# ScalarE's hi parts first in each slot, VectorE's lo parts last, and the first batch's keys on GpSimd: a pooled attention with a gated expert layer

## The chip, the core and the metric

The kernel runs on one core of one Trainium2 chip. The metric is the device time of one launch in microseconds (us), the median of several runs. All work goes through five engines, each with an instruction queue that it works off strictly in order: PE (TensorE: matrix products and transpositions into PSUM; its weight loads are listed as PEld), DVE (VectorE), ACT (ScalarE, which also issues some DMAs), POOL (GpSimd) and SP (SyncE, which here only issues DMAs).

## The reference

Attention against keys and values that are averaged over 8 positions (72 pooled keys for 576 queries, 8 batches, 8 heads, 64 wide), and then a gated layer without a nonlinearity:

```python
k_p = k.reshape(B, H, Sp, pool, D).mean(axis=3)
v_p = v.reshape(B, H, Sp, pool, D).mean(axis=3)
scores = scale * np.matmul(q, k_p.transpose(0, 1, 3, 2))
scores = scores - np.max(scores, axis=-1, keepdims=True)
attn = np.exp(scores)
attn = attn / (np.sum(attn, axis=-1, keepdims=True) + 1e-09)
attn_out = np.matmul(attn, v_p)
x = attn_out.transpose(0, 2, 1, 3).reshape(B * S, H * D)      # 4608 x 512
a = x @ w1;  b = x @ w2                                       # 512 -> 1024
out = (a * b @ w3) @ w_out                                    # 1024 -> 1024 -> 512
```

All inputs and outputs are float32.

## The kernel before

**Splitting.** A float32 operand of a product is kept as a hi part (a rounded copy, nearly always written by ACT) and a lo part (the operand minus hi, written by DVE, sometimes by GpSimd). A product is three passes: hi x hi, hi x lo, lo x hi. So nearly each result that PE leaves in PSUM is read twice, by ACT for hi and by DVE for lo.

**Stages.** (1) *The opening* builds W = w3 x w_out (its first half) in 8 steps, `w_block(v)` and `w_mm(s, ...)`. The weights arrive as 32-bit halves of 64-bit numbers: `high` (ACT) and `low` plus the two operations of `conv_b` (DVE) rebuild a float32 in the tile `wt`; `w_turn` transposes on PE, and a hi/lo pair `hl` is made of the transposed w3 and of w_out. Beside it runs the attention of chunk 0. (2) *The middle* goes over 12 chunks of 384 tokens. For chunk m and column block j of 4, `a_mm` and `b_mm` are 12 products each (w1 and w2), `a_post` and `b_post` make g = a x b and its hi part, `g_lo` the lo part, and `out_mm` multiplies by W into three accumulators `o`, which `out_post(m, t)` copies out through `ob` and stores as a partial result. In the same slots stands the attention of the next chunk. (3) *The tail* adds the other half of the hidden width by another scheme (lines 730 and 797) and stores the output.

**Attention of one chunk n**, tile t of 96 or 128 tokens: `s_mm` (scores of four heads each, `att` in PSUM), `soft1` (maximum, subtraction, exponential; where the pair (n, t) is in SOFT_ACT, ACT does the subtraction and the sum too), `soft2` (division), `soft3` (the 8 keys that don't fit 64, as tile R in hi and lo), `pt_mm` and `ptr_mm` (transpositions), `pt_post` and `ptr_post` (their evictions PTh, PTl, PTr), `av_mm` (times v) and `av_post` (xT hi and lo for the next layer, and a copy `xs` that is stored for the tail). PSUM tiles named `att` share three buffers; a buffer is given again when its last reader is through. For batch b, `load_k` and `prep_k` sum the keys over 8 positions, by a tree of three additions on GpSimd or, for the pairs in K_DVE, by one reduction on DVE; `kt_mm` and `kt_post` make `kbd` of them; `prep_v`, `prep_v2`, `prep_vr` and `prep_vr2` do the same for v, where `prep_vr` holds three ACT operations that wait for GpSimd's sum, and `prep_v2` an ACT copy `vbd` that GpSimd's queue then waits for. `st` (three buffers) takes the loads of k and v, `qs` (four) those of q, and `tr_q` on DVE frees a `qs`.

**What sets the order.** A plan written as numbers. `at(kind, k, fn, ...)` puts a call at slot k. Calls are run sorted by whole slot, then by kind in the order L (loads), P (work on ACT, DVE and GpSimd), M (main products), A (attention products), then by the fraction of k. So each engine's queue holds the work of slot after slot, and within a slot's P part the fraction decides. M0 is the slot of `a_mm` of chunk 0, and a chunk has IA = 12 slots. `plan_att`, `plan_kv` and `plan_q` place one chunk's attention, one batch's keys and values, and one chunk's queries:

```python
plan.append((k // 1, "LPMA".index(kind), k % 1, len(plan), fn, args))
...
for _, _, _, _, fn, args in sorted(plan, key=lambda x: x[:4]):
    fn(*args)
```

An instruction that reads a PSUM tile on one engine also waits for an earlier reader of the tile on another engine.

Of the kernel before, what the change touches and what calls it, by code (L numbers as in the profile page):

```python
# [19 lines left out]
def kernel(  # L20
# [170 lines left out]

    def w_block(v):


# [1 line left out]
        if new:
            w_tiles(v)
            r3, z3 = stage["w3", v]
            ro, zo = stage["wo", v]
            high(raw["w3", v], z3)  # L200
            low(raw.pop(("w3", v)), r3)
            high(raw["wo", v], zo)
        if old:
            s = v - 2
            sub(wo[s][1], f(stage["wo", s][0]), f(wo[s][0]))
        if new:
            if v > 0:
                low(raw["wo", v], ro)
            conv_b(r3, z3)
        if mid:  # L210
            ps = w_turn(v - 1)
            w3t[v - 1] = hl(cell, 8 + (v - 1) % 4)
            nc.scalar.copy(out=w3t[v - 1][0], in_=ps)
        if new:
            if v == 0:
                low(raw["wo", v], ro)
            conv_b(ro, zo)
        if mid:
            wo[v - 1] = hl(cell, v - 1)
            nc.scalar.copy(out=wo[v - 1][0], in_=f(stage["wo", v - 1][0]))  # L220
        if mid:
            nc.vector.tensor_tensor(out=w3t[v - 1][1], in0=ps, in1=f(w3t[v - 1][0]), op=ALU.subtract)
# [267 lines left out]
    def soft1(n, t, half):  # L490
# [9 lines left out]
        if (n, t) not in SOFT_ACT:  # L500
            nc.vector.tensor_tensor(  # L501
                out=E[:nt, hs], in0=sv,
                in1=mx[:nt, hs].unsqueeze(2).broadcast_to([nt, 4, KP]), op=ALU.subtract)
            nc.scalar.activation(out=E[:nt, hs], in_=E[:nt, hs], func=AF.Exp, scale=-1.0)  # L504
            nc.vector.reduce_sum(out=sm[:nt, hs], in_=E[:nt, hs], axis=AX.X)  # L505
            return
# [50 lines left out]
    def pt_post(n, t):  # L557
# [26 lines left out]
    def av_post(n, pr):  # L584
# [235 lines left out]
    def plan_att(n, k, s_at, pt_at, av_at):  # L820


        for t in range(len(tok_tiles(n))):
# [98 lines left out]
    for u in range(8):
# [4 lines left out]
        at("A", k + 2, w2_turn, u)  # L927
        at("P", k + 3, w2_split, u)
        at("A", k + 4, w2_mm, u)
        at("P", k + 5, w2_post, u)  # L930
# [79 lines left out]
```

## Time and profile before

| | us |
|---|---|
| median of 3 runs | 932.97 (930.59 to 935.16) |
| the profiled execution | 934.14 |
| its span, first to last instruction | 932.0 |
| opening, to the first `a` product | 121.4 |
| chunk 0 of the middle | 54.6 |
| chunks 1 to 11 | 478 |
| tail | 278 |
| PE busy | 797.7 (86%) |
| DVE busy | 615.4 (66%) |
| ACT busy | 340.8 (37%) |
| POOL busy | 240.7 (26%) |

The mean granted TensorE clock is 0.937 of full speed. One load of a key pair is 288 KB, one step of W loads 512 KB of w3 and 512 KB of w_out, one query DMA is 48 KB. In the profile, an engine is busy while it works on an instruction; a wait is named by what released it, and since queues are in order, a wait delays all that stands behind it on its engine. A wait on an engine that others don't wait for costs nothing.

### The profile page before, as it was taken

The numbers are of one execution on the slowest core, as the hardware profiler recorded it, in microseconds if no ns is written. First come the engines' busy times: TensorE is split into PE (matmuls) and PEld (weight loads), VectorE is DVE, ScalarE is ACT, GpSimd is POOL, SyncE is SP. The second block draws the span as 40 slices with busy tenths as digits, with TensorE's granted clock in tenths as the row PEclk, the third lists the DMA queues.
The fourth block names the chain that finished last, engine by engine and source line by source line (L and its number), as shares of the span: only waits on it lengthen the run. The fifth ranks groups of instructions, "written<-read, shape, count | busy, mean of one in ns | idle before, by whom it ended". The sixth has DMA issues, their size and how long they took to land.

```text
span 932.0 us, 12974 instructions
## 1 busy us (share of the span) xinstructions
PE 797.7 (86%) x4512; PEld 720.2 (77%) x4512; DVE 615.4 (66%) x1273; ACT 340.8 (37%) x863; POOL 240.7 (26%) x295
## 2 busy tenths in 40 slices
PE   3466667898889897979997988998899999999998
PEld 3344556887778796868886877887898998998996
DVE  2968578656565756485765676657777687677644
ACT  2244452453444443433443443544222122122111
POOL 2644137344151342422251100000211211211211
PEclk7767879799899998999998999999899999999999
DMA  8954523444444444424433312253141341341122
GB/s 242 242 125 139 149 56 87 112 129 117 102 113 106 130 119 112 116 89 107 133 80 90 95 56 80 74 192 128 44 141 58 108 142 57 108 142 57 58 91 79
DMA packets 131840, 102.56 MB, mean 110 GB/s; under 512 B 82624, under 2 KB 103104, under 8 KB 130752
## 3 DMA queue, kind: packets, MB, share of 16 engines
q1 hardware_dynamic: 116800, 81.82, 32.6%
q10 hardware_dynamic: 14976, 19.93, 6.0%
q8 instruction: 35, 0.57, 0.3%
q14 instruction: 29, 0.24, 0.1%
HBM read 72.35 MB, written 29.36 MB: 109 GB/s over the span
## 4 chain that ended last, share of the span: by engine, by line
PE 40%; DVE 28%; ACT 14%; DMA 9%; issue 4%; POOL 2%; ACTq 2%; SPq 1%; DVEq 0%; POOLq 0%
PE ps L730 19%; PE att L797 11%; PE att L282 3%; ACT E L504 2%; DMA st<-in_v_dram 2%; PE a L609 2%; DVE E L501 2%; DVE mx L499 2%; DVE PTl L566 2%; DVE sm L505 2%; PE o L644 2%; DVE xT L126 2%; DVE gl L635 2%; DVE a L629 2%; DMA qs<-in_q_dram 2%
## 5 line engine op out<-in xcount | busy, mean ns | idle before, releaser
L730 PE MATMUL ps<-xo,sw 128*128 128x288 f32 x1344 | 182.3, 297 | 3.5 <-ACT m L749 3.5
L730 PEld LDWEIGHTS ps<-xo,sw 128*128 128x128 f32 x1344 | 181.7, 190 | 4.4 <-ACT m L749 3.7
L742 POOL TENSOR_TENSOR g<-g,u 128x288 f32<-128x288 f32 x48 | 40.8, 866 | 339.9 <-DVE u L123 339.9
L644 PE MATMUL o<-W,gh 128*128 128x512 f32 x288 | 95.6, 414 | 27.6 <-ACT ob L649 26.3
L609 PE MATMUL a<-xT,hl 128*128 128x384 f32 x576 | 115.8, 350 | 2.7 <-ACT hl L181 1.5
L441 POOL TENSOR_TENSOR st<-st 72x512 f32<-72x512 f32 (+1 forms) x54 | 74.2, 1374 | 166.5 <-DMA st<-in_v_dram 56.1
L609 PE MATMUL b<-xT,hl 128*128 128x384 f32 x576 | 113.2, 344 | 2.1 <-DVE a L629 1.2
L609 PEld LDWEIGHTS a<-xT,hl 128*128 128x128 f32 x576 | 105.5, 197 | 5.2 <-POOL hl L182 1.9
L609 PEld LDWEIGHTS b<-xT,hl 128*128 128x128 f32 x576 | 100.8, 192 | 3.1 <-POOL hl L182 1.6
L644 PEld LDWEIGHTS o<-W,gh 128*128 128x128 f32 x288 | 51.6, 192 | 41.4 <-ACT ob L649 32.7
L797 PE MATMUL att<-W,gh 128*128 128x512 f32 x256 | 80.2, 394 | 0.0
L483 PE MATMUL att<-kbd,qT 128*128 128x144 f32 (+1 forms) x320 | 60.6, 314 | 21.5 <-ACT xs L594 10.1
L483 PEld LDWEIGHTS att<-kbd,qT 128*128 128x128 f32 (+1 forms) x320 | 50.6, 195 | 30.6 <-ACT xs L594 11.3
L504 ACT ACTIVATE E<-E 128x288 f32<-128x288 f32 (+1 forms) x70 | 31.1, 444 | 107.7 <-DVE E L501 103.1
L123 DVE TENSOR_TENSOR u<-u,ps 128x288 f32<-128x288 f32 x112 | 49.0, 451 | 18.1 <-PE ps L730 17.9
L505 DVE TENSOR_REDUCE sm<-E 128x4 f32<-128x288 f32 (+1 forms) x70 | 31.6, 451 | 41.7 <-ACT E L504 41.7
L644 PE MATMUL o<-W,gl 128*128 128x512 f32 x144 | 58.1, 403 | 0.8 <-DVE gl L635 0.8
L749 ACT COPY m<-ps 128x288 f32<-128x288 f32 x32 | 12.8, 400 | 123.4 <-PE ps L730 110.0
L797 PEld LDWEIGHTS att<-W,gh 128*128 128x128 f32 x256 | 48.0, 188 | 10.9
L566 DVE TENSOR_TENSOR PTl<-att,PTh 128x512 fp32r<-128x512 f32 (+1 forms) x40 | 25.4, 636 | 43.7 <-ACT PTh L565 43.5
L126 DVE TENSOR_TENSOR xT<-att,xT 128x384 fp32r<-128x384 f32 x48 | 26.7, 556 | 41.0 <-ACT xT L589 40.6
L797 PE MATMUL att<-W,gl 128*128 128x512 f32 x128 | 50.5, 394 | 0.0
(126 smaller groups left out, 1421.5 us busy)
## 6 DMA issues: line engine op xcount, KB each, us to landing
raw<-in_moe_w_dram SPq DMA_DIRECT2D x32, 512.0 KB
st<-in_k_dram SPq DMA_DIRECT2D x32, 288.0 KB
pd<-ob ACTq DMA_DIRECT2D x36, 256.0 KB
x<-xd SPq DMA_DIRECT2D x8, 1152.0 KB
part<-pd SPq DMA_DIRECT2D x36, 256.0 KB
out_dram<-ob SPq DMA_DIRECT2D x36, 256.0 KB
st<-in_v_dram SPq DMA_DIRECT2D x32, 256.0 KB
qs<-in_q_dram SPq DMA_DIRECT2D x128, 48.0 KB
```

Source lines behind the costliest of these rows:

```text
L123: eng.tensor_tensor(out=out, in0=a, in1=b, op=ALU.add)
L126: eng.tensor_tensor(out=out, in0=a, in1=b, op=ALU.subtract)
L441: nc.gpsimd.tensor_tensor(out=t[:, :, 0:4], in0=t[:, :, 0:4], in1=t[:, :, 4:8], op=ALU.add)
L483: nc.tensor.matmul(out=ps[:nt, 2 * KP * j:2 * KP * (j + 1)], lhsT=qT[n][:, pr, off:off + nt], rhs=kbd[b % 2][:, pr], start=True, stop=True,)
L504: nc.scalar.activation(out=E[:nt, hs], in_=E[:nt, hs], func=AF.Exp, scale=-1.0)
L505: nc.vector.reduce_sum(out=sm[:nt, hs], in_=E[:nt, hs], axis=AX.X)
L566: nc.vector.tensor_tensor(out=lo, in0=pv[:, :, :nt], in1=f(hi), op=ALU.subtract)
L609: nc.tensor.matmul(out=o, lhsT=w12[j, w][sw][:, kt * P:(kt + 1) * P], rhs=x[sx][:, kt], start=(i == 0), stop=(i == 3 * NK - 1))
L644: nc.tensor.matmul(out=oacc[m][t], lhsT=(gh, gl)[sg][:, c], rhs=W[0, j][sw_], start=(j == 0 and i == 0), stop=(j == NA - 1 and i == 2))
L730: nc.tensor.matmul(out=ps[:, :HS], lhsT=w[a][:, kt * P:(kt + 1) * P], rhs=x[b][:, kt], start=(j == 0), stop=(j == 5))
L742: nc.gpsimd.tensor_tensor(out=d, in0=d, in1=tmp[into], op=ALU.mult)
L797: nc.tensor.matmul(out=oacc["b", no], lhsT=G[no][a][:, j], rhs=W[1, j][b], start=(j == 0 and n == 0), stop=(j == 3 and n == 2))
```

## The change

In every slot, the P part is put in another order, and some calls are cut in two so that it can be:

- `av_post` now holds the hi copy, the `xs` copy and its store; the lo part is a call of its own, `av_lo`, behind them. `pt_post` keeps the hi copy, `pt_lo` is new. `b_post` is now the product alone, `g_hi` and `g_lo` follow. `soft3` keeps ACT's copies, `soft4` has DVE's subtractions, and `soft2`, `soft3` and `soft4` of a tile stand in one slot. The two sums of E per tile become one, in `soft2`.
- `w_block` is reordered: ACT's hi copies of the step before first, then per matrix the lo part and the rebuilding. The `high` operations go into `w_high`, a slot earlier.
- Key pair 1 of batch 0 leaves K_DVE, so all four are summed on GpSimd. The first three key loads stand behind four steps of W's loads, queries behind the fifth step, the fourth key pair and the values later.
- Numbers: M0 is a slot later (K0 + 3), attention of chunk 0 starts at slot 10 in place of 7, that of chunk 1 moves as well; `out_post` of a chunk's second and third accumulator moves from one and two slots behind the first to 0.4 and 1; `w2_turn` and `w2_split` are one slot later, `w2_mm` and `w2_post` two.

```diff
-    K_DVE = [(0, 1), (1, 1)]
+    K_DVE = [(1, 1)]
...
+    def w_high(v):
+        w_tiles(v)
+        high(raw["w3", v], stage["w3", v][1])
+        high(raw["wo", v], stage["wo", v][1])
...
     def soft2(n, t):
...
+        if (n, t) not in SOFT_ACT:
+            nc.vector.reduce_sum(out=sm[:nt], in_=E[:nt], axis=AX.X)
...
+    def soft4(n, t):
+        nt = tok_tiles(n)[t][2]
+        R = Rt[n, t][:nt]
         for dup in range(2):
-            nc.vector.tensor_tensor(
-                out=R[:nt, :, :, dup, 1], in0=er, in1=f(R[:nt, :, :, dup, 0]), op=ALU.subtract)
+            sub(R[:, :, :, dup, 1], rest_keys(n, t), f(R[:, :, :, dup, 0]))
...
         nc.scalar.copy(out=xh, in_=ps)
-        sub(xl, ps, f(xh))
+        stage["xl", n, pr] = xl, ps, f(xh)
...
+    def av_lo(n, pr):
+        sub(*stage.pop(("xl", n, pr)))
...
-            at("P", k + av_at[pr] + 1, av_post, n, pr)
+            at("P", (k + av_at[pr]) // 1 + 1.1, av_post, n, pr)
+            at("P", (k + av_at[pr]) // 1 + 1.5, av_lo, n, pr)
...
-    M0 = K0 + 2
+    M0 = K0 + 3
...
-    plan_kv(0, -2, 1.25, 2.6, 5, 8, 10)
-    plan_q(0, -1, 1, 3, 1)
-    plan_att(0, 7, [0, 2, 4], [4, 6, 8], [11, 11.5, 12, 12.5])
+    plan_kv(0, (0, 0.1, 0.2, 5, 6, 7, 8), (4, 5, 6, 7.5, 9, 10, 11.5), 8, 13, 14)
+    plan_q(0, 1, 1, 5, 1)
+    plan_att(0, 10, [0, 2, 4], [4, 6, 8], [10, 10.5, 11, 11.5])
...
         for t in range(3):
-            at("P", m0 + IA + 3 + t, out_post, m, t)
+            at("P", m0 + IA + (3, 3.4, 4)[t], out_post, m, t)
```

**DVE in the opening.** The rows are a line of the code, an operation, and tile out<-in; `wt` are rebuilt weights, `km` the summed keys, `hl` a hi/lo pair. Before, behind step 0 (rows of `raw_164` and `raw_166`) and up to step 1's end:

```order
L177 SCALAR_TENSOR_TENSOR wt_233<-wt_234,wt_233 128x512
L398 TENSOR_REDUCE km_247<-st_224 72x128
L166 TENSOR_SCALAR wt_235<-raw_168 128x512
L166 TENSOR_SCALAR wt_233<-raw_170 128x512
L175 SCALAR_TENSOR_TENSOR wt_235<-wt_237,wt_235 128x512
```

and now:

```order
L177 SCALAR_TENSOR_TENSOR wt_223<-wt_224,wt_223 128x512
L166 TENSOR_SCALAR wt_225<-raw_168 128x512
L175 SCALAR_TENSOR_TENSOR wt_225<-wt_227,wt_225 128x512
L177 SCALAR_TENSOR_TENSOR wt_225<-wt_227,wt_225 128x512
L126 TENSOR_TENSOR hl_258<-att_253,hl_258 128x512
L166 TENSOR_SCALAR wt_223<-raw_170 128x512
```

The reduction over a key load is gone from between steps 0 and 1, and the lo part of the transposed w3 stands between the two matrices of the step.

**ACT at the first AV tile of a chunk** (chunk 2, `xT` and `xs` of its tile 0, `vbd` of batch 2). Before:

```order
L630 CAST gh_1723<-a_1696 128x384
L589 CAST xT0_1727<-att_1718 128x384
L594 COPY xs_869<-att_1718 128x384
L596 DMA xd1_121<-xs_869 128x384
L453 CAST vbd0_0_95<-vm_1424 64x4x64 x2
```

and now:

```order
L448 CAST vbd0_0_95<-vm_1420 64x4x64
L285 COPY ws_1719<-att_1703 128x512
L593 CAST xT0_1721<-att_1698 128x384
L598 COPY xs_901<-att_1698 128x384
L600 DMA xd1_121<-xs_901 128x384
L528 CAST R_1733<-E_1642 128x8x8 x2
L641 CAST gh_1736<-a_1677 128x384
```

The first of the two `vbd` copies stands ahead of the tile's copies and of `gh`, which it stood behind.

**ACT at the copies out of a chunk** (`ob`, chunk 0; `vrh` and `vrm` are the casts of `prep_vr`). Before:

```order
L462 ACTIVATE vrh_1550<-vrh_1550,msk_101 128x128
L463 ACTIVATE vrm_1549<-vrm_1549,msk_101 128x128
L649 COPY ob_1580<-o1_1187 128x512
L650 DMA pd1_129<-ob_1580 128x512
L619 COPY a_1583<-a_1557 128x384
L414 ACTIVATE kbd0_93<-att_1570 64x4x72 x2
L181 CAST hl_1592<-att_1575 128x512
L649 COPY ob_1616<-o2_1188 128x512
```

and now:

```order
L457 ACTIVATE vrh_1545<-vrh_1545,msk_101 128x128
L458 ACTIVATE vrm_1544<-vrm_1544,msk_101 128x128
L660 COPY ob_1552<-o1_1181 128x512
L661 DMA pd1_129<-ob_1552 128x512
L660 COPY ob_1574<-o2_1182 128x512
L661 DMA pd2_130<-ob_1574 128x512
L626 COPY a_1577<-a_1556 128x384
```

The third copy follows the second at once; both still stand behind the casts of `prep_vr`.

More of the change, by code (lines that the diff above doesn't have):

```diff
@@ L190, in w_tiles @@
         stage["w3", s] = stage["w3t"][s % 4], f(stage["w3t"][4 + s % 4])
+    def w_high(v):
+        w_tiles(v)
+        high(raw["w3", v], stage["w3", v][1])
+        high(raw["wo", v], stage["wo", v][1])
     def w_block(v):
         new, mid, old = v < NJ, 0 <= v - 1 < NJ, 0 <= v - 2 < NJ
[L196 to L202, printed above, removed]
+        if mid:
+            ps = w_turn(v - 1)
+            w3t[v - 1] = hl(cell, 8 + (v - 1) % 4)
+            nc.scalar.copy(out=w3t[v - 1][0], in_=ps)
+            wo[v - 1] = hl(cell, v - 1)
+            nc.scalar.copy(out=wo[v - 1][0], in_=f(stage["wo", v - 1][0]))
         if old:
@@ L206, in w_block @@
         if new:
-            if v > 0:
-                low(raw["wo", v], ro)
-            conv_b(r3, z3)
+            low(raw.pop(("w3", v)), stage["w3", v][0])
+            conv_b(*stage["w3", v])
         if mid:
-            ps = w_turn(v - 1)
-            w3t[v - 1] = hl(cell, 8 + (v - 1) % 4)
-            nc.scalar.copy(out=w3t[v - 1][0], in_=ps)
+            sub(w3t[v - 1][1], ps, f(w3t[v - 1][0]))
         if new:
[L215 to L222, printed above, removed]
+            low(raw.pop(("wo", v)), stage["wo", v][0])
+            conv_b(*stage["wo", v])
     def warm(n):
@@ L565, in pt_post, with pt_lo @@
         nc.scalar.copy(out=hi, in_=pv[:, :, :nt])
-        nc.vector.tensor_tensor(out=lo, in0=pv[:, :, :nt], in1=f(hi), op=ALU.subtract)
+        stage["ptl", n, t] = lo, pv[:, :, :nt], f(hi)
+    def pt_lo(n, t):
+        sub(*stage.pop(("ptl", n, t)))
     def ptr_post(n, t):
@@ L626, in b_post, with g_hi @@
         g, ps = gt[m, j]
+        nc.vector.tensor_tensor(out=g, in0=ps[:, :CH], in1=g, op=ALU.mult)
+        gt[m, j] = g
+    def g_hi(m, j):
+        g = gt[m, j]
         gh = p2.tile([P, CH], F32R, tag="gh", name="gh")
         gl = p2.tile([P, CH], F32R, tag="gl", name="gl")
-        nc.vector.tensor_tensor(out=g, in0=ps[:, :CH], in1=g, op=ALU.mult)
         nc.scalar.copy(out=gh, in_=g)
@@ L827, in plan_att @@
                 at("P", x + half + 1, soft1, n, t, half)
-            at("P", x + 3, soft2, n, t)
-            at("P", x + 4, soft3, n, t)
+            at("P", x + 3.1, soft2, n, t)
+            at("P", x + 3.3, soft3, n, t)
+            at("P", x + 3.8, soft4, n, t)
             x = k + pt_at[t]
@@ L871 @@
     for s in range(NJ + 2):
+        if s < NJ:
+            at("P", F0 + 2 * (s - 2) - (0.2 if s else 0), w_high, s)
         at("P", F0 + 2 * (s - 2) + 0.6, w_block, s)
@@ L901 @@
             at("P", k + 2, b_post, m, j)
-            at("P", k + 2.5, g_lo, m, j)
+            at("P", k + 2.35, g_hi, m, j)
+            at("P", k + 2.9, g_lo, m, j)
             at("M", k + 5, out_mm, m, j)
         for t in range(3):
-            at("P", m0 + IA + 3 + t, out_post, m, t)
+            at("P", m0 + IA + (3, 3.4, 4)[t], out_post, m, t)
     for n in range(1, NCH):
@@ L916 @@
         if b == 1:
-            plan_kv(b, 7, 1.5, 2.4, 14, k, k + 1)
-        else:
-            plan_kv(b, k - 22, 1.75, 2.6, k - 9, k - 4, k - 3)
+            load = [10.5 + 1.5 * i for i in range(7)]
+            plan_kv(b, load, [x + 2.5 for x in load], 19, k + 1, k + 2)
+        else:
+            load = [k - 22 + 1.75 * i for i in range(7)]
+            plan_kv(b, load, [x + 2.6 for x in load], k - 9, k - 4, k - 3)
     for u in range(8):
@@ L926 @@
         at("P", k + 1, w2_conv2, u)
[L927 to L930, printed above, removed]
+        at("A", k + 3, w2_turn, u)
+        at("P", k + 4, w2_split, u)
+        at("A", k + 6, w2_mm, u)
+        at("P", k + 7, w2_post, u)
         if u % 2:
-            at("P", k + 7, w2_store, u // 2)
+            at("P", k + 8, w2_store, u // 2)
     for qq in range(4):
```

31 lines of the change are left out of this document (15 added, 16 removed).

## The prediction

> **What bounds the kernel now.** I read the engine totals first, then the same totals by stage, then who waits for whom inside each stage. A row of the second view is a stretch in us from the span's start, its length, the busy time of PE, PEld, DVE, ACT and POOL (with instruction counts), the granted clock, the DMA share and GB/s.
>
> ```profile
> PE 797.7 (86%) x4512; PEld 720.2 (77%) x4512; DVE 615.4 (66%) x1273; ACT 340.8 (37%) x863; POOL 240.7 (26%) x295
> 0.00:121.40 121.40, 66.05 (x276) 52.44 (x277) 78.67 (x134) 47.84 (x151) 45.25 (x57) 0.73 0.68 176
> 121.40:176.00 54.60, 40.85 (x201) 35.99 (x201) 42.64 (x72) 22.67 (x59) 29.97 (x30) 0.84 0.30 76
> 176.00:654.00 478.00, 418.59 (x2334) 379.40 (x2332) 303.45 (x665) 205.67 (x496) 112.13 (x144) 0.97 0.40 110
> 654.00:932.00 278.00, 272.19 (x1704) 252.39 (x1704) 190.59 (x405) 64.67 (x157) 53.36 (x64) 0.98 0.27 88
> ```
>
> No engine is full before 654 us. The opening (W, first attention) ends at 121.4 us, where the first `a` product starts; it has DVE busy 78.67 us, the most of any engine, so 42.7 us of DVE's time there are waits. Chunk 0 of the middle takes 54.6 us, the other eleven 478/11 = 43.5 us each. From 654 us on PE is busy 272.19 of 278.00 and the change leaves that code alone: nothing to win there. In the 478 us PE is idle 478.00 - 418.59 = 59.4 us, and these are the causes (engine, line, waited for: us in total, times, longest):
>
> ```profile
> PE o L644 <- ACT ob L649: 26.3, 13, 5.0
> PE att L483 <- ACT xs L594: 5.3, 3, 1.8
> PE att L553 <- ACT xs L594: 5.1, 6, 1.5
> ...
> PE att L234 <- DVE wt L177: 3.8, 2, 1.9
> PE att L282 <- ACT PTr L570: 3.0, 2, 1.5
> ```
>
> All are waits of PE for an eviction that stood late in ACT's or DVE's queue: order, not throughput. That is what the change edits.
>
> **The opening: -9 us.** Rows here and below are start, us, engine, line, operation, [idle before <- releaser].
>
> ```profile
> 13.29 0.66 ACT L161 ACTIVATE wt<-raw 128x512 f32<-128x512 f32 x1 [1.01 <-DMA raw<-in_moe_w_out_dram]
> 15.73 4.37 SPq L370 DMA_DIRECT2D qs<-in_q_dram  x4
> 21.90 1.87 DVE L398 TENSOR_REDUCE km<-st 72x128 f32<-72x1024 f32 x1 [13.08 <-DMA st<-in_k_dram]
> 26.85 1.09 PE L234 MATMUL att<-ident,wt 128*128 128x128 f32 x4 [17.68 <-DVE wt L177]
> 29.23 1.02 DVE L381 STREAM_TRANSPOSE qT<-qs 128x384 f32<-128x384 f32 x2
> 37.37 0.38 DVE L166 TENSOR_SCALAR wt<-raw 128x512 int32<-128x512 int32 x1
> 66.80 1.93 DVE L398 TENSOR_REDUCE km<-st 72x128 f32<-72x1024 f32 x1
> ```
>
> DVE stands 13.08 us in front of the sum of key pair 1, with steps 1 and 2 of W already landed (13.29), and PE idles 17.68 us behind it. With the pair on GpSimd DVE goes straight on: steps 1 and 2 end near 19 us instead of 37. What is late next: `tr_q` stays ahead of step 3, and the queries are now issued on SP behind four steps of W, three key pairs and W's step 4. Three steps landed by 13.3 us, so one costs 4.4 us at most; step 3, three key pairs (288 KB each against a step's 1024) and step 4 make that 26, and eight query DMAs at the 4.37 us for four seen here make 35. I take 29, since the 13.3 holds the start-up too and issue overlaps transfer. Step 3 then begins near 30 us, where before it began at 37.37: 7.4 us earlier. After that DVE meets two more waits: the highs of step 6 stand on ACT behind the `vr` cast, and pair 1 of batch 1 is still summed on DVE (66.80 in the old run), its load now behind 16 query DMAs after `vr`. Later, attention of chunk 0 starts three slots later against W, so more of it lies between W and the first product, but `hi` first and `lo` last takes most of the ACT round trips out of it. Ends: the whole 17.68 us gained, or 4 us lost (M0 is a slot later, and a slot is 43.5/12 = 3.6 us). Nearest to the 7.4 us of the row, with a little of the round trips: -9.
>
> The tree sum of the moved pair is GpSimd work, and there is a place where that hurts, a DVE operation on the same shape taking 1.65 us after 0.68:
>
> ```profile
> 154.81 0.68 DVE L175 SCALAR_TENSOR_TENSOR wb<-wb 128x512 int32<-128x512 int32 x1
> 155.00 1.64 POOL L182 TENSOR_TENSOR hl<-wb,hl 128x512 fp32r<-128x512 f32 x1 [2.21 <-ACT hl L181]
> 155.53 1.65 DVE L177 SCALAR_TENSOR_TENSOR wb<-wb 128x512 int32<-128x512 int32 x1
> ```
>
> One pair moved is one such doubling or two, 1 to 2 us, and DVE loses its own 1.87 us: zero net. [...]
>
> **Chunk 0: -5 us.** The two stalls below are of the same kind: ACT's `xs` copy waited until DVE had read the same PSUM tile for `xT` lo. Now `xs` follows the hi copy at once.
>
> ```profile
> 163.54 1.33 PE L483 MATMUL att<-kbd,qT 128*128 128x144 f32 x4 [3.97 <-ACT xs L594]
> 167.20 0.53 PE L578 MATMUL att<-PTh,vbd 128*128 128x192 f32 x1 [2.34 <-ACT xs L594]
> ```
>
> They are 6.3 us, and the clock of 0.84 over 54.6 us costs up to 8.7 more. Against that, two tiles of chunk 1's softmax move into this stage. Ends -12 and 0; I take -5.
>
> **The eleven chunks after it: -32 us.** (a) The `ob` waits, 26.3 us. One of the three large places, in order of time:
>
> ```profile
> 202.62 0.47 ACT L589 CAST xT<-att 128x384 fp32r<-128x384 f32 x1
> 203.13 0.56 DVE L126 TENSOR_TENSOR xT<-att,xT 128x384 fp32r<-128x384 f32 x1 [0.96 <-ACT xT L589]
> 203.72 0.48 ACT L594 COPY xs<-att 128x384 f32<-128x384 f32 x1 [0.62 <-DVE xT L126]
> 204.60 0.83 ACT L453 CAST vbd<-vm 64x256 fp32r<-64x256 f32 x2 [0.40 <-ACT xs L594]
> 205.08 0.77 POOL L454 TENSOR_TENSOR vbd<-vm,vbd 64x256 fp32r<-64x256 f32 x1 [12.64 <-ACT vbd L453]
> 208.48 1.26 SPq L422 DMA_DIRECT2D st<-in_v_dram  x2
> 209.83 11.02 SPq L370 DMA_DIRECT2D qs<-in_q_dram  x16
> 220.95 5.41 SPq L435 DMA_DIRECT2D st<-in_v_dram  x8
> 230.22 1.26 POOL L441 TENSOR_TENSOR st<-st 128x512 f32<-128x512 f32 x1 [10.71 <-DMA qs<-in_q_dram]
> 232.84 0.30 ACT L460 CAST vrh<-vrm 128x128 fp32r<-128x128 f32 x1 [5.63 <-POOL vrm L443]
> 233.77 0.56 ACT L649 COPY ob<-o 128x512 f32<-128x512 f32 x1
> 234.39 1.22 PE L644 MATMUL o<-W,gh 128*128 128x512 f32 x2 [5.02 <-ACT ob L649]
> 237.08 1.22 PE L644 MATMUL o<-W,gh 128*128 128x512 f32 x2 [1.05 <-ACT ob L649]
> 365.70 0.74 PE L644 MATMUL o<-W,gh 128*128 128x512 f32 x2 [3.61 <-ACT ob L649]
> 499.80 0.85 PE L644 MATMUL o<-W,gh 128*128 128x512 f32 x2 [3.81 <-ACT ob L649]
> ```
>
> `vbd` on ACT frees GpSimd, which frees the buffer that SP's `v` load waits for, behind which 16 query DMAs and the `vr` load are queued; `vr`'s sum and cast then stand on ACT ahead of the second `ob`. That cast still does (0.10 against 0.40 in the slot). But `vbd` now stands ahead of the `xT`/`xs` pair of its slot, not behind it: 2.0 us earlier by these rows (202.62 to 204.60), some 3 with the `gh` copy and its wait on DVE, which stood ahead of that and now stand behind; and the rest of the chain moves with it. And the third `ob` follows the second at once, so the 1.05 goes. Each place keeps about 2 us of 4 to 6. Third `ob` a slot earlier ends the waits elsewhere. 26.3 becomes about 6: -20. (b) `w2_turn` and `w2_mm` one and two slots later: the 3.8 and 3.0 go, -7. (c) The `xs` waits, 5.3 + 5.1, go, but the PSUM tiles (three `att` buffers) are now held until the lo parts at the slot's end, and `soft1` stands ahead of the last `av_post`. From the rows, hi 0.47, xs 0.48, lo 0.56 and the softmax of one half between them make the transposition after the last AV product wait about 1.5 us, once in each chunk: 16 in place of 10.4, +5. (d) The clock: (1 - 0.97) x 478 = 14 us of lost speed. I leave 4:
>
> ```profile
> 545.99 0.73 PE L644 MATMUL o<-W,gh 128*128 128x512 f32 x2 [2.17 <-ACT ob L649]
> 550.00:575.00 25.00, 20.65 (x115) 18.91 (x115) 15.88 (x37) 10.92 (x29) 0.00 (x0) 0.90 0.15 50
> ```
>
> A stall of 2.17 us was followed by a stretch at 0.90, so the 2 us that stay may cost 1.5 us each three times: -10. [...] Sum: -20 - 7 + 5 - 10 = -32. Ends: -46 (no new waits, no old ones) and -10 (all freed time but (a)'s half taken by new ones).
>
> **Edits at zero.** The two sums of `E` in one:
>
> ```profile
> L505 DVE TENSOR_REDUCE sm<-E 128x4 f32<-128x288 f32 (+1 forms) x70 | 31.6, 451 | 41.7 <-ACT E L504 41.7
> ```
>
> Two of 451 ns become one of 451 to 902, and the 41.7 us in which DVE waited for the exponential go. DVE is not what PE waits for by throughput here (303.45 of 478), so this has no term of its own; if that cover is gone it shows in (c). `g_hi`, `g_lo` and the R parts have two slots until their product. The loads' new numbers for batches 2 to 7 are the old ones.
>
> **Sum.** -9 - 5 - 32 = -46 against the profiled execution's 934.1 us gives 888; the median of the runs is 1.2 us lower, so 887.
>
> **Rivals.** *The opening gives nothing* (queries, `vr` and pair 1 of batch 1 hand the 9 us back; the 66.80 row speaks for it): 896. *Waits are exchanged*: DVE's work of the slots around AV, b, softmax and four lo parts, fills those slots, and only the opening, chunk 0 and a third of the 32 stay: 909. *Near the floor*: all of 17.68, half more of chunk 0 and 46: 862 to 868. *The change is not seen*, because SP's chain (28 us from `vbd` to `vr`) paces chunks whatever ACT does; against it, seven of the thirteen `ob` waits are not at that chain: 933. *Slower*: the three `att` buffers. If each of the four AV tiles of a chunk, not only the last, makes PE wait 1.5 us, that is 3 x 1.5 x 12 = 54 us more, 941; it decides once hi, xs and lo of a tile take longer than about one slot, 3.6 us, the time until a buffer is wanted again. Against it: `xs` no longer waits for DVE, which alone took 0.62 us per tile.
>
> **How the numbers follow.** Forecast 0.50, opening gives nothing 0.14, exchanged 0.14, floor 0.09, not seen 0.05, slower 0.08. Half a percent, about 4.7 us, is what a measurement can tell: faster 0.87, same 0.05, slower 0.08. The range takes in floor to a little past exchanged: 862 to 918, the outer ends of the opening and of the 32 included; the four faster cases hold 0.87, and their tails beyond it some 0.07.
>
> **What would show it.** Right: DVE has no wait near 13 us long at the start; the first `a` product starts at 105 to 118 us; `ob` waits under 10 us in all and no pair of them above 3; no `xs` <- `xT` wait on ACT; stage four again 278 us. Wrong: transpositions or scores waiting for lo parts for more than 20 us, the first product at 121 us or later, or `vr` still 5 us behind PE.

## The result, and the profile after

The changed kernel takes 871.7 us (median of 3 runs, 870.44 to 873.28) against 932.97: a ratio of 0.9345, 95% interval 0.9301 to 0.9389. The forecast was 887 us, 862 to 918.

The engine totals, and then the same four stages as before (start and end in us, length, busy time of PE, PEld, DVE, ACT and POOL with instruction counts, granted clock, DMA share, GB/s):

```profile
PE 776.7 (89%) x4512; PEld 709.2 (82%) x4512; DVE 610.2 (70%) x1237; ACT 334.8 (38%) x863; POOL 242.7 (28%) x298
0.00:117.60 117.60, 64.55 (x269) 51.60 (x269) 76.97 (x135) 48.24 (x146) 45.56 (x60) 0.75 0.70 181
117.60:165.90 48.30, 37.71 (x209) 35.54 (x208) 37.72 (x66) 21.93 (x66) 28.21 (x30) 0.88 0.36 89
165.90:592.00 426.10, 403.31 (x2334) 370.84 (x2332) 303.51 (x632) 199.96 (x496) 115.61 (x144) 1.00 0.44 122
592.00:869.90 277.90, 271.13 (x1704) 251.23 (x1704) 192.01 (x406) 64.65 (x157) 53.32 (x64) 0.99 0.26 90
```

The span is 62.1 us shorter: the opening 3.8, chunk 0 6.3, chunks 1 to 11 51.9, the tail 0.1. In the eleven chunks PE executes the same 2334 instructions; its idle time fell from 59.4 to 22.8 us and its busy time by 15.3, with the granted clock at 1.00. Of the causes of PE's idle time in that stretch (engine, line, waited for: us in total, times, longest) these are the rows that answer to the old list:

```profile
PE att L478 <- DVE E L496: 4.5, 5, 1.4
PE att L478 <- DVE xT L126: 3.2, 4, 1.0
PE o L655 <- ACT ob L660: 1.1, 2, 0.7
PE att L229 <- DVE E L496: 0.5, 1, 0.5
```

Of the `ob` waits (26.3) 1.1 us are left; the `xs` waits (10.4) are gone, and so are the two waits at w2's transposition and product (6.8).

### The profile page after: what moved, and what is told of

The parts are those of the page before. It is cut to its first block, busy times and chain, and to the rows that moved or that the text cites. A ratio compares the mean times of both kernels' runs of the same rounds, so it can differ in the third digit from the quotient of the medians.

```text
span 869.9 us, 12921 instructions
## 1 busy us (share of the span) xinstructions
PE 776.7 (89%) x4512; PEld 709.2 (82%) x4512; DVE 610.2 (70%) x1237; ACT 334.8 (38%) x863; POOL 242.7 (28%) x298
## 4 chain that ended last, share of the span: by engine, by line
PE 53%; DVE 19%; DMA 12%; ACT 6%; SPq 3%; issue 3%; POOL 3%; ACTq 1%; DVEq 0%; POOLq 0%
PE ps L741 20%; PE att L808 12%; PE b L616 5%; PE a L616 5%; DMA qs<-in_q_dram 3%; PE o L655 3%; DMA st<-in_v_dram 3%; PE att L478 3%; PE att L277 2%; SPq L430 2%; DVE E L517 2%; DMA raw<-in_moe_w_out_dram 1%; DVE mx L494 1%; DVE E L496 1%; DMA raw<-in_moe_w_dram 1%
## 5 line engine op out<-in xcount | busy, mean ns | idle before, releaser
L616 PE MATMUL a<-xT,hl 128*128 128x384 f32 x576 | 113.0, 345 | 0.0
L616 PEld LDWEIGHTS a<-xT,hl 128*128 128x128 f32 x576 | 101.9, 192 | 1.5 <-ACT a L626 0.7
L655 PE MATMUL o<-W,gh 128*128 128x512 f32 x288 | 92.7, 403 | 2.4 <-ACT gh L641 1.3
L478 PE MATMUL att<-kbd,qT 128*128 128x144 f32 (+1 forms) x320 | 57.1, 301 | 29.4 <-DVE E L496 9.9
L478 PEld LDWEIGHTS att<-kbd,qT 128*128 128x128 f32 (+1 forms) x320 | 46.8, 184 | 38.1 <-ACT E L503 9.9
L499 ACT ACTIVATE E<-E 128x288 f32<-128x288 f32 (+1 forms) x70 | 31.1, 445 | 79.5 <-DVE E L496 79.2
L123 DVE TENSOR_TENSOR u<-u,ps 128x288 f32<-128x288 f32 x112 | 49.0, 451 | 17.9 <-PE ps L741 17.3
L670 PE MATMUL o<-hl 128*128 128x512 f32 x72 | 29.7, 542 | 26.9 <-DVE hl L126 26.8
L494 DVE TENSOR_REDUCE mx<-att 128x4 f32<-128x288 f32 (+1 forms) x80 | 35.9, 450 | 19.1 <-PE att L478 19.0
```

The lines of the kernel that those rows point to most:

```text
L123: eng.tensor_tensor(out=out, in0=a, in1=b, op=ALU.add)
L478: nc.tensor.matmul(out=ps[:nt, 2 * KP * j:2 * KP * (j + 1)], lhsT=qT[n][:, pr, off:off + nt], rhs=kbd[b % 2][:, pr], start=True, stop=True,)
L494: nc.vector.tensor_reduce(out=mx[:nt, hs], in_=sv, axis=AX.X, op=ALU.min)
L616: nc.tensor.matmul(out=o, lhsT=w12[j, w][sw][:, kt * P:(kt + 1) * P], rhs=x[sx][:, kt], start=(i == 0), stop=(i == 3 * NK - 1))
L655: nc.tensor.matmul(out=oacc[m][t], lhsT=(gh, gl)[sg][:, c], rhs=W[0, j][sw_], start=(j == 0 and i == 0), stop=(j == NA - 1 and i == 2))
L670: nc.tensor.matmul(out=wacc[0][it], lhsT=w3t[s][sa][:, it * P:(it + 1) * P], rhs=wo[s][sb], start=(s == 0 and i == 0), stop=(s == NJ - 1 a ...
```

## The experiments

Stage figures are of one profiled execution each; medians are of 4 to 8 runs, those of the first two rows of 3. "Chunk 1 starts" is the start of its first `a` product. The stretch ends 11.6 us after the tail's first product of each kernel, so the gain in it is 51.4 here for the 51.9 of the rounded edges above.

| kernel | chunk 1 starts | chunks 1 to 11 | PE idle there | PE busy there | median |
|---|---|---|---|---|---|
| before | 176.0 | 477.6 | 59.0 | 418.6 | 932.97 |
| changed | 165.9 | 426.2 | 22.9 | 403.3 | 871.7 |
| old opening | 166.7 | 425.9 | 23.0 | 402.9 | 875.8 |
| old `ob` slots | 164.4 | 426.9 | 21.9 | 405.0 | 870.4 |
| AV lo ahead of `xs` | 168.5 | 437.2 | 31.0 | 406.2 | 887.5 |
| old w2 slots | 167.0 | 457.3 | 43.4 | 413.9 | 905.9 |
| `vbd` back | 167.2 | 429.0 | 23.8 | 405.2 | 876.2 |
| `gh` first | 164.5 | 445.7 | 34.7 | 410.9 | 890.4 |
| old softmax | 170.1 | 432.3 | 25.2 | 407.0 | 880.4 |
| `gh`, `vbd`, `ob` old together | 172.1 | 426.8 | 23.6 | 403.3 | 879.2 |
| before + new w2 slots | 181.6 | 468.8 | 48.0 | 420.9 | 927.9 |
| queries later | 167.3 | 427.7 | 22.4 | 405.3 | 875.4 |
| opening re-ordered | 159.5 | 428.7 | 23.1 | 405.7 | 870.6 |
| the same, `vr` behind | 150.6 | 427.3 | 22.8 | 404.5 | 857.6 |

How much two executions of the same code differ ahead of chunk 1 can be read from this table. Two kernels that change nothing ahead of it (old `ob` slots, old w2 slots) reach it at 164.4 and 167.0, the changed one at 165.9. The new w2 slots change nothing ahead of it either, yet "before + new w2 slots" reaches it at 181.6 (its first `a` product starts at 126.72) where the kernel before has 176.0 (121.46). So a difference of less than some 6 us at that place, in one execution each, shows nothing by itself. In the eleven chunks the spread is smaller: the last three kernels and the old opening, whose edits all lie ahead of chunk 1, take 425.9 to 428.7 us there against 426.2.

**The opening undone.** In the changed kernel:

```
-    K_DVE = [(1, 1)]
+    K_DVE = [(0, 1), (1, 1)]
-    plan_kv(0, (0, 0.1, 0.2, 5, 6, 7, 8), (4, 5, 6, 7.5, 9, 10, 11.5), 8, 13, 14)
+    plan_kv(0, [-2 + 1.25 * i for i in range(7)], [0.6 + 1.25 * i for i in range(7)], 5, 8, 10)
     (also plan_q(0), plan_att(0), M0 = K0 + 2, the old w_block without w_high,
      batch 1's loads, the slot of chunk 1's queries)
```

> The changed kernel with the opening of the kernel before: both key pairs on DVE, the loads, queries and chunk 0's attention in their old slots, M0 a slot earlier, the W block in its old order; the order within slots and all numbers of the middle stay new (chunk 1's score slots too). Theory: the opening gave 3.8 us, by fewer waits of DVE, so the first a product comes back to about 121 us, chunk 0 and the eleven chunks stay as in the changed kernel, 874 to 878 us. Rival 1: the new order within slots alone is what shortened the opening (the new numbers bring nothing): first product at 117 to 118 and 870 to 873. Rival 2: the old early attention collides with the split eviction order: above 880.

Measured: 875.8 us, ratio to before 0.9382 (0.9353 to 0.9411), which overlaps the changed kernel's interval. DVE waits for the key load as it did before the change (first row, of DVE's waits in the opening), and yet the opening and chunk 0 are short:

```profile
DVE km L399 <- DMA st<-in_k_dram: 12.3, 1, 12.3
0.00:113.92 113.92, 62.75 (x268) 50.30 (x269) 75.20 (x124) 44.55 (x139) 43.12 (x57) 0.75 0.75 185
113.92:166.72 52.80, 42.20 (x210) 38.50 (x209) 42.12 (x77) 25.19 (x74) 29.75 (x31) 0.82 0.34 86
```

The first `a` product starts at 113.9 us and chunk 1 at 166.7, not at the 121.4 and 176.0 of before: in these executions 9.3 of the 10.1 us that the changed kernel gains up to chunk 1 come without any of the new opening. By the medians, too, 57 of the 61 us of the whole change are there without it. The total lies in the theory's range, but the time stands where rival 1 put it. What is left to shorten the opening is the order within slots, which also runs in chunk 0's attention, and the later slots of chunk 1's scores, which this kernel keeps too. The two were not run apart, and the 7.5 us at the first product are not far above the spread.

**The slots of the `ob` copies undone.**

```
-            at("P", m0 + IA + (3, 3.4, 4)[t], out_post, m, t)
+            at("P", m0 + IA + (3, 4, 5)[t], out_post, m, t)
```

> The changed kernel with the copies of a chunk's second and third accumulator back at one and two slots behind the first. Theory of the prediction (the earlier vbd copy frees the chain of GpSimd, v load and vr, and most of the ob waits go with it): the third copy's own waits return, ob waits 8 to 12 us in chunks 1 to 11, no pair at the large places above 3, with some lost clock 880 to 888. Rival 1: the slot of the copies is all that counts: ob waits 20 us or more, 895 to 912. Rival 2: the copies have slack now: ob waits under 3 us, 870 to 874.

Measured: 870.4 us (0.9344, 0.9307 to 0.9381): no difference. PE's `ob` waits did come back, but other waits shrank by as much, and the stretch is 426.9 us long. Rival 2 has the time right and the reason wrong (it had `ob` waits under 3 us).

```profile
PE o L655 <- ACT ob L660: 7.3, 7, 2.4
```

A sum of waits by name is not a gain: the idle time of the stretch (21.9 against 22.9) is.

**The AV lo part ahead of `xs`.**

```
         nc.scalar.copy(out=xh, in_=ps)
-        stage["xl", n, pr] = xl, ps, f(xh)
+        sub(xl, ps, f(xh))
```

> The changed kernel with the lo part of an AV tile back between its hi copy and its xs copy. Theory: the xs copy again waits for DVE's reading of the same PSUM tile, some 20 us of waits on ACT in all, and PE's waits for a free att buffer come back, 5 to 10 us in chunks 0 to 11, with lost clock 877 to 885. Rival: xs stood late because of the whole slot order, not of the lo part: waits on ACT come back but PE waits no longer than now, 870 to 874.

Measured: 887.5 us (0.9517, 0.9486 to 0.9547), 11.0 us longer in the eleven chunks. The waits of PE and of ACT in chunks 1 to 11:

```profile
PE att L478 <- ACT xs L598: 12.8, 12, 2.1
ACT xs L598 <- DVE xT L126: 34.5, 40, 3.4
```

The theory holds, 2.5 us past its upper end: ACT waits at 40 tiles for DVE, and 12 times PE waits for the buffer.

**w2's slots undone.**

```
-        at("A", k + 3, w2_turn, u)
-        at("P", k + 4, w2_split, u)
-        at("A", k + 6, w2_mm, u)
+        at("A", k + 2, w2_turn, u)
+        at("P", k + 3, w2_split, u)
+        at("A", k + 4, w2_mm, u)
     (and w2_post two slots, w2_store one slot earlier)
```

> The changed kernel with w2's work back in its old slots (transposition one slot, product two slots earlier). Theory of the prediction's term (b): PE's waits for the rebuilt weights (3.8 us before) and for an att buffer at w2_mm (3.0) come back, with a little lost clock 876 to 881. Rival: those two waits came from DVE and ACT being late in the slot, which the new order cured without the new slots: 870 to 873.

Measured: 905.9 us (0.9702, 0.9668 to 0.9737). More than half of the whole gain goes with five numbers, far past the theory. Neither of the two waits named came back; these did (PE's two, then DVE's):

```profile
PE att L478 <- DVE qT L376: 20.4, 7, 4.1
PE o L655 <- ACT ob L660: 7.4, 5, 2.6
DVE hl L182 <- ACT hl L181: 43.3, 8, 9.2
```

One of the eight places, in three queues (DVE; ACT; PE):

```profile
226.48 0.69 DVE L182 TENSOR_TENSOR hl<-att,hl 128x512 fp32r<-128x512 f32 x1 [7.80 <-ACT hl L181]
221.77 0.30 ACT L455 CAST vrh<-vrm 128x128 fp32r<-128x128 f32 x1 [3.43 <-POOL vrm L438]
222.70 0.56 ACT L660 COPY ob<-o 128x512 f32<-128x512 f32 x1
223.66 0.59 ACT L660 COPY ob<-o 128x512 f32<-128x512 f32 x1 [0.40 <-ACT ob L660]
225.87 0.58 ACT L181 CAST hl<-att 128x512 fp32r<-128x512 f32 x1
229.61 0.79 PE L478 MATMUL att<-kbd,qT 128*96 128x144 f32 x2 [4.10 <-DVE qT L376]
```

`w2_split` writes the hi part on ACT and the lo part on DVE. ACT is late, since `vr`'s cast waited for GpSimd and two `ob` copies, `a` and `kbd` follow; DVE, whose turn is come, stands 7.80 us in front of a subtraction of 0.69. Three query transpositions, a softmax and a product stand behind it in DVE's queue, and PE waits 4.10 us for the second half of the queries. In the changed kernel the same place has (ACT, ACT, DVE):

```profile
214.95 0.30 ACT L455 CAST vrh<-vrm 128x128 fp32r<-128x128 f32 x1 [1.80 <-POOL vrm L438]
219.46 0.59 ACT L181 CAST hl<-att 128x512 fp32r<-128x512 f32 x1
220.72 0.68 DVE L182 TENSOR_TENSOR hl<-att,hl 128x512 fp32r<-128x512 f32 x1
```

A slot later the softmax and all but one of the query transpositions are through ahead of the lo part, and it finds the hi part written.

**`vbd` back behind the first AV tile.**

```
-            at("P", v_at + 0.5 * hf, prep_v2, b, hf)
+            at("P", v_at + 0.12 + 0.38 * hf, prep_v2, b, hf)
```

> The changed kernel with the first vbd copy of a batch back behind the first AV tile's hi and xs copies (0.12 instead of 0 in its slot); nothing else. Theory (vbd paces the chain to vr, 6 us between the two places here): GpSimd's key sum, the v load and vr come 4 to 6 us later, the ob waits at three places come back with 3 to 5 us each, with lost clock 882 to 892. Rival: the order of the ob copies alone took the waits away and the chain has slack: 870 to 874, ob waits under 3 us.

Measured: 876.2 us (0.9396, 0.9366 to 0.9425), 2.8 us longer in the eleven chunks, hardly more than the spread there; `ob` waits 1.5. That decides nothing on the chain, for the edit did not delay it: `vbd` came late (GpSimd's row), but the key sum now ran ahead of it in GpSimd's queue, so the `v` load was issued no later (SP's row: 21.8 us after chunk 1's start, 25.5 in the changed kernel).

```profile
195.27 0.73 POOL L449 TENSOR_TENSOR vbd<-vm,vbd 64x256 fp32r<-64x256 f32 x1 [10.85 <-ACT vbd L448]
189.05 2.23 SPq L417 DMA_DIRECT2D st<-in_v_dram  x2
```

**`gh` first in its slot.**

```
-            at("P", k + 2.35, g_hi, m, j)
+            at("P", k + 2, g_hi, m, j)
```

> The changed kernel with ACT's gh copy back at the head of its slot, right behind DVE's product a x b that it reads. Theory now: neither the vbd copy nor the slot of the ob copies took the ob waits away (876 and 870 with each undone), but ACT's queue, which stood 53.8 us waiting for the product before and 14.3 after; with gh first, ACT waits 40 us more in chunks 1 to 11, everything behind it is late, and PE's waits on ACT (ob, R, PTr, xs) grow by 10 to 25 us: 882 to 905. Rival: ACT has slack for those waits: 870 to 875.

Measured: 890.4 us (0.9541, 0.9509 to 0.9574), all of it in the eleven chunks. ACT's wait for the product grew as expected:

```profile
ACT gh L641 <- DVE a L634: 48.9, 39, 4.4
164.45:610.10 445.65, 410.92 (x2334) 376.48 (x2332) 307.27 (x632) 200.73 (x495) 116.12 (x144) 0.98 0.42 117
```

PE's idle time grew by 11.8 us, spread over a dozen causes with no single wait above 2.6 us, and its busy time by 7.6, with the clock at 0.98. The time lies in the theory's range, the place only in part: of the waits on ACT that it named, `ob` and `PTr` grew by 3.9 us together and `R` and `xs` not at all, while PE's waits on DVE grew by more.

**The old softmax.** The sum per half tile again behind its exponential, `soft2` at x + 3, `soft3` and `soft4` at x + 4:

```
-            at("P", x + 3.1, soft2, n, t)
-            at("P", x + 3.3, soft3, n, t)
-            at("P", x + 3.8, soft4, n, t)
+            at("P", x + 3, soft2, n, t)
+            at("P", x + 4, soft3, n, t)
+            at("P", x + 4, soft4, n, t)
```

> The changed kernel with the softmax as before: a sum per half tile right behind its exponential, division at the head of its slot, R's hi and lo parts at the head of the next slot. Theory of the prediction (zero term, DVE has cover): DVE again waits some 37 us for the exponential, PE does not notice, 870 to 874. Rival: a part of the gain that no term of mine holds sits here; DVE reaches the lo parts and the products late, PE's waits on DVE grow: 880 to 895.

Measured: 880.4 us (0.9433, 0.9401 to 0.9465): 6.1 us longer in the eleven chunks; the 4.2 us up to chunk 1 are within what two executions differ there. The rival, at its lower end.

**`gh`, `vbd` and `ob` undone together** (the three edits above in one kernel).

> The changed kernel with three edits undone together: gh first in its slot, vbd behind the first AV tile's copies, ob copies at one and two slots distance. Theory: each of them alone could keep the ob copies in time, so that undoing one shows little; together the ob waits come back, 15 to 26 us, with lost clock 895 to 915. Rival: they add up, that is e6's loss and 4 us more for vbd and nothing for ob: under e6 + 7.

Measured: 879.2 us (0.9411, 0.9378 to 0.9445). Both expectations fail: the losses do not add up, and the `ob` waits do not come back (5.0 us). The chunks 1 to 11 take 426.8 us, as in the changed kernel, and what is lost lies before chunk 1 (6.2 us in this execution, near the spread there; the median lost 7.5), for a reason that stays open. `gh` first costs 19.5 us in the eleven chunks with the new `ob` and `vbd` places; together with the old ones it costs nothing against the changed kernel, though ACT waits for the product nearly as long (44.4 us). Which of the two makes the difference was not run.

**w2's slots alone, on the kernel before.** The five numbers of the change, all else old.

> The kernel before with one part of the change alone: w2's transposition and split one slot later, its product two slots later. Theory now: undoing this cost 34 us because DVE stands before the lo part of w2's split until ACT, behind the vr casts and two ob copies, has written the hi part (43.3 us of such waits with the old slots, 21.8 in the kernel before, 1.3 after), and the transposition of queries and the softmax stand behind it; so done alone it takes 18 to 32 us from the kernel before, 900 to 915, and DVE's waits for ACT's hl fall under 5 us in chunks 1 to 11. Rival (prediction's term b: only PE's 3.8 and 3.0): 924 to 929.

Measured: 927.9 us (0.9937, 0.9906 to 0.9969). The rival is right: 8.8 us in the eleven chunks, 5 us in all. DVE's waits for ACT's `hl`, 21.8 us before, fell to 1.5, but ACT is nearly as late as it was, with 12.3 us of waits for `vr`'s sum where it had 14.3 (stretch; PE's and ACT's waits):

```profile
181.57:650.40 468.83, 420.88 (x2334) 383.54 (x2332) 307.22 (x665) 204.85 (x496) 112.75 (x144) 0.96 0.40 112
PE o L644 <- ACT ob L649: 19.0, 11, 4.2
ACT vrh L460 <- POOL vrm L443: 12.3, 3, 4.5
```

So in the eleven chunks w2's numbers bring 8.8 us alone, everything else without them 20.3 (477.6 to 457.3), and both together 51.4. Neither is worth its share. With w2's numbers alone PE still stands 19.0 us before the `ob` copies; with everything else alone DVE stands 43.3 us before w2's lo parts. That each of the two stalls hides what the other's removal is worth fits these rows, but was not followed wait by wait.

**Queries of chunk 0 later.** The opening of the changed kernel still holds these waits, each behind the other (DVE's, then the two of ACT that cause the second and third):

```profile
24.91 0.58 DVE L376 STREAM_TRANSPOSE qT<-qs 128x384 f32<-128x384 f32 x1 [6.60 <-DMA qs<-in_q_dram]
45.62 0.69 DVE L175 SCALAR_TENSOR_TENSOR wt<-wt 128x512 int32<-128x512 int32 x1 [5.30 <-ACT wt L161]
58.72 0.69 DVE L175 SCALAR_TENSOR_TENSOR wt<-wt 128x512 int32<-128x512 int32 x1 [4.90 <-ACT wt L161]
71.92 1.87 DVE L393 TENSOR_REDUCE km<-st 72x128 f32<-72x1024 f32 x1 [4.29 <-DMA st<-in_k_dram]
44.06 0.82 ACT L409 ACTIVATE kbd<-att 64x288 f32<-64x288 f32 x2 [8.17 <-PE att L402]
57.12 0.30 ACT L455 CAST vrh<-vrm 128x128 fp32r<-128x128 f32 x1 [3.24 <-POOL vrm L438]
```

```
-    plan_q(0, 1, 1, 5, 1)
+    plan_q(0, 1, 1, 8.7, 0.05)
```

> The changed kernel with one number moved: the four query transpositions of chunk 0 stand on DVE behind W step 4 instead of between steps 2 and 4. Theory: DVE's 9.3 us of waiting for queries in the opening go, step 3 starts at about 19 instead of 29 us, and half of that stays at the first product: 865 to 869. Rival: the next late thing (ACT stands 8.2 us before kbd until the last key pair is loaded and summed, behind 16 query DMAs) takes it all back: 870 to 873.

Measured: 875.4 us (0.9381, 0.9360 to 0.9403), chunk 1 at 167.3. Nothing gained: DVE's waits for ACT's `wt` grew from 10.2 to 15.5 us, and ACT's wait before `kbd` from 8.2 to 15.7. The rival, 2.4 us past its far side.

**The whole opening re-ordered.**

```
-    K_DVE = [(1, 1)]
+    K_DVE = []
-    plan_kv(0, (0, 0.1, 0.2, 5, 6, 7, 8), (4, 5, 6, 7.5, 9, 10, 11.5), 8, 13, 14)
-    plan_q(0, 1, 1, 5, 1)
+    plan_kv(0, (0, 0.1, 0.2, 3.1, 6, 7, 8), (4, 5, 6, 7, 9, 10, 13.3), 8, 13, 14.2)
+    plan_q(0, 3.3, 0.3, 8.7, 0.05)
```

> The changed kernel with the opening re-ordered in five numbers: query transpositions behind W step 4, key pair 3 loaded behind W's step 5 and ahead of the queries, the queries after it, the vr casts 1.8 slots later, pair 1 of batch 1 on GpSimd. Theory: the four waits behind each other in the opening (queries 9.3 us and pair 4.3 on DVE; 5.3 and 4.9 in which DVE waits for ACT behind kbd and vr) go, and about half of their 24 us arrives at the first product: it starts at 102 to 110 us, 857 to 866. Rival: the loads bind (DMA share 0.98 in the first slices) or DVE's busy time does, and no more than 3 us is left of it: 868 to 873.

Measured: 870.6 us (0.9332, 0.9311 to 0.9352), first product at 110.8, chunk 1 at 159.5. The total is the rival's, for a reason that it did not have: all four waits are gone, and one took their place (GpSimd, ACT, DVE):

```profile
61.00 1.26 POOL L436 TENSOR_TENSOR st<-st 72x512 f32<-72x512 f32 x1 [8.97 <-DMA st<-in_k_dram]
66.16 0.30 ACT L455 CAST vrh<-vrm 128x128 fp32r<-128x128 f32 x1 [13.72 <-POOL vrm L438]
67.35 0.37 DVE L126 TENSOR_TENSOR R<-E,R 128x64 fp32r<-128x64 f32 x2 [17.66 <-ACT R L528]
```

GpSimd's first key sum of batch 1, whose load is queued behind chunk 1's queries, stood ahead of `vr`'s sum; ACT's cast waited for that, `R` stood behind the cast, and DVE behind `R`.

**`vr` behind.** On top of it:

```
-    plan_kv(0, (0, 0.1, 0.2, 3.1, 6, 7, 8), (4, 5, 6, 7, 9, 10, 13.3), 8, 13, 14.2)
+    plan_kv(0, (0, 0.1, 0.2, 3.1, 6, 7, 8), (4, 5, 6, 7, 9, 10, 15.2), 8, 14.9, 16.5)
-            plan_kv(b, load, [x + 2.5 for x in load], 19, k + 1, k + 2)
+            plan_kv(b, load, (15.5, 16, 17, 18, 19, 20.5, 22), 19, k + 1, k + 2)
```

> The re-ordered opening of the run before, in which one stall was left (DVE stood 17.7 us before R's lo part, behind ACT's vr cast, behind GpSimd's vr sum, which I had put behind the first key sum of batch 1 and so behind its late load): now vbd and the vr casts of batch 0 stand two slots later, and batch 1's key sums behind vr. Theory: that stall falls under 4 us, 10 to 14 us arrive at the first product, which starts at 96 to 102 us, and the total is 854 to 862. Rival: the opening's end is set by DVE's own 80 us of work, by late loads of batch 1 or by GpSimd's sums that lie beside DVE's two-input operations (1.6 us instead of 0.69 there), so that less than half arrives: 864 to 870.

Measured: 857.6 us (855.68 to 858.73), ratio to before 0.9200 (0.9176 to 0.9225), clear of the changed kernel's interval: the best version here.

```profile
0.00:102.28 102.28, 62.76 (x269) 50.86 (x269) 85.83 (x133) 47.69 (x145) 51.86 (x63) 0.78 0.78 204
```

The first product starts at 102.28, at the late edge of the theory's range, the total lies in it, and DVE's longest wait in the opening is 2.5 us. DVE is now busy 85.8 of 102.3 us.

## Why the forecast came out as it did, step by step

**Direction and range held; the gain was 61 us where 46 were summed.** 871.7 us lies nearer to the rival "near the floor" (862 to 868) than to the forecast. That it lies in the range at all is partly luck: the eleven chunks gave 20 us more than their term and stand past its outer end (51.9 against 46), and the opening gave less than its own. Of the marks named, these came: no DVE wait near 13 us, the first product at 117.6 (the last edge of 105 to 118), `ob` waits of 1.1, no `xs` wait on ACT, the same tail.

**Opening, -9 forecast, -3.8 measured, less than two executions of the same code differ there.** The local step was right: W's step 3 begins at 29.3 us where 30 was worked out, 8 us earlier than before.

```profile
29.28 0.42 DVE L166 TENSOR_SCALAR wt<-raw 128x512 int32<-128x512 int32 x1
```

What failed is the step from there to the first product: the waits that follow took the 8 us back (two were named; `kbd`'s 8.17 us on ACT, behind the late fourth key pair, was not). The kernel with the old opening shows that the new one brings nothing measurable up to chunk 1, so that the gain there belongs to what that kernel keeps. The rival in which the opening gives nothing had this part.

**Chunk 0, -5 forecast, -6.3 measured.** Right in size, and the two `xs` stalls (6.3 us) are gone. But other waits on DVE took their place (5.4 us for `E`, 3.5 for the queries, 1.7 for the `xT` lo part), so PE's idle time fell only from 13.8 to 10.6 us; its busy time fell by the other 3.1. Since chunk 0 takes 48.3 to 50.3 us in kernels that do not touch it, a match to about one us is chance.

**Eleven chunks, -32 forecast, -51.9 measured** (with the profile's edges as above). Term by term:

- (a) `ob`: -20 forecast by 26.3 to 6; 26.3 to 1.1. The chain was advanced more than the "some 3 us" worked out, since `vbd` also stands ahead of w2's copy `ws`, for which ACT waits (ACT; SP; GpSimd, in the changed kernel):

```profile
187.19 0.41 ACT L448 CAST vbd<-vm 64x256 fp32r<-64x256 f32 x1
191.13 0.59 ACT L285 COPY ws<-att 128x512 f32<-128x512 f32 x1 [3.53 <-PE att L277]
191.43 1.26 SPq L417 DMA_DIRECT2D st<-in_v_dram  x2
212.27 1.29 POOL L436 TENSOR_TENSOR st<-st 128x512 f32<-128x512 f32 x1 [6.96 <-DMA qs<-in_q_dram]
```

  From chunk 1's start the `v` load is issued at 25.5 us (before: 208.48 - 176.0 = 32.5), and `vr`'s sum begins at 46.4 (before 54.2). The forecast rested this term on `vbd`'s new place. That place is not enough: with w2's slots undone `ws` stands ahead of `vbd` again, and the `v` load is issued at 32.4 us (199.36 - 167.0), as late as before. Nor do w2's slots alone do it: on the kernel before, `vbd` stays behind the `xs` copy, and the load is issued at 31.2 (212.76 - 181.6). The kernel with w2's slots undone has (ACT; GpSimd):

```profile
190.29 0.59 ACT L285 COPY ws<-att 128x512 f32<-128x512 f32 x1 [1.20 <-PE att L277]
219.11 1.28 POOL L436 TENSOR_TENSOR st<-st 128x512 f32<-128x512 f32 x1 [7.79 <-DMA qs<-in_q_dram]
```

  There `vr`'s sum begins at 52.1 us, and the `ob` waits are 7.4 us, not 26.3. So a chain nearly as late as the old one does not bring the old `ob` waits back in the new order. How much of them it made in the kernel before is not shown: no run delayed it alone.
- (b) w2, -7: as an edit by itself it is about that size (8.8 measured on the kernel before). The step that failed is to add it to the others, beside which it is worth 31.1. It was sized by PE's two waits; the time that DVE stood before w2's lo part was in the old trace (below) and carried no term, because DVE was not the bound.

```profile
DVE hl L182 <- ACT hl L181: 21.8, 6, 7.2
```

- (c) `xs`: +5 forecast, some -7 measured: 10.4 us of waits replaced by 3.2, four waits of at most 1.0 and not one of 1.5 in each chunk. The tiles held until the lo part cost next to nothing, so the rival in which they decide (941) had no ground. Undoing the order costs 11.0 us there.
- (d) clock: -10 forecast, -15.3 measured (PE's busy time; the granted clock went from 0.97 to 1.00).
- Zero terms: the softmax's slots and sums are worth 6.1 us in the eleven chunks, so "no term of its own" was wrong. `g_hi`'s place had none either, and undone alone costs 19.5.

Undone one at a time, the edits cost 0.7, 2.8, 6.1, 11.0, 19.5 and 31.1 us in the eleven chunks (the first two about as small as the spread there), 71.2 together, where the change brought 51.4. A sum of separate terms was the wrong form for queues that wait for each other.

## What to carry to other kernels

Before a step is priced by the bound engine's waits, list for each engine the instructions at which it stands longest and what is queued behind them: a lo part of 0.69 us that waited up to 7.2 us for another queue, on an engine at 66%, was the largest single lever. In-order queues that read each other's results have to be put in order together; one edit of a pair may show a sixth of the pair's gain, and undoing one may cost more than half of it. A stall taken out of an opening pays only once the last of the stalls behind it is out: here the change's own re-ordering and two more brought nothing that shows clearly in the total, and the last one, on top of them, 13 us.

## What the runs showed of the hardware

**PE's busy time grew with its idle time, but one stall of 2.62 us cost no clock.** Over the eleven chunks PE's busy time for the same 2334 instructions rises on the whole with its idle time: 403 to 407 us at 22 to 31 us idle, 410.9 at 34.7, 413.9 at 43.4, 420.9 at 48.0, 418.6 at 59.0. The granted clock there falls from 1.00 to 0.96 and 0.97. It is not a strict rule: the last two stand in the other order. The forecast charged a stall of about 2 us with a stretch at low clock. In the kernel before, that stall was followed by another, and the 5 us around them already had a clock of 0.81 (PE rows, then the stretch):

```profile
545.99 0.73 PE L644 MATMUL o<-W,gh 128*128 128x512 f32 x2 [2.17 <-ACT ob L649]
548.41 0.85 PE L483 MATMUL att<-kbd,qT 128*128 128x144 f32 x2 [1.22 <-DVE qT L381]
545.00:550.00 5.00, 2.80 (x10) 2.46 (x11) 3.73 (x9) 1.63 (x4) 0.00 (x0) 0.81 0.14 52
```

In the changed kernel a longer one was followed by 7 us at full clock:

```profile
502.64 0.36 PE L583 MATMUL att<-PTl,vbd 128*128 128x192 f32 x1 [2.62 <-ACT R L528]
502.00:509.00 7.00, 6.36 (x47) 6.36 (x48) 3.44 (x9) 3.37 (x10) 0.00 (x0) 1.00 0.18 59
```

So the granted clock stayed at 1.00 behind 2.62 us of idle time in one kernel and was 0.81 around 2.17 us, the longest idle time on end there, in the other. The length of the single stall does not tell the two apart. What does is not shown: no run here varied a stall's length or place by itself.

**Key sums on GpSimd were not free beside W.** With the queries out of the way, W's rebuilding and GpSimd's key sums ran at the same time, and some DVE operations of 0.65 to 0.69 us took 1.63 to 1.76 (DVE, GpSimd, in the re-ordered opening):

```profile
17.66 1.76 DVE L126 TENSOR_TENSOR hl<-wt,hl 128x512 fp32r<-128x512 f32 x1
17.18 1.70 POOL L436 TENSOR_TENSOR st<-st 72x512 f32<-72x512 f32 x1 [11.76 <-DMA st<-in_k_dram]
```

DVE's busy time up to the first product is 85.8 us in the best kernel against 77.0 in the changed one, with one reduction fewer. In the changed kernel three of the four key sums of batch 0 (17.9 to 25.9 us) lay mostly in DVE's wait for queries (18.3 to 24.9), and "zero net" held there: DVE's busy time in the opening is 77.0 us against 78.7 before. In the re-ordered opening the four such DVE operations ahead of 31 us each overlap one of the four key additions over 512 elements on GpSimd, which took 1.60 to 1.74 us; in the changed kernel the two that lay whole in DVE's wait for queries took 1.26. That the two engines held each other up is a reading of this overlap; no run varied it by itself.
